# Another order of all steps of the recurrence in a fused RWKV-7 and low-rank mixer kernel

## The chip, the cores and the metric

One Trainium2 chip, of which the kernel uses one core. The metric is the device time of one execution in microseconds (us).

## The reference

Inputs r, k, v, w, a, b have the shape (4, 8, 768, 40): batch, heads, time steps, head size. Per batch and head a 40 x 40 state is carried through the 768 steps, and what comes out is mixed over time by a low-rank pair U, V and over channels by a two-layer network, with a residual sum around each:

```python
for t in range(S):
    y[:, :, t] = einsum('bhd,bhde->bhe', rt, state)
    Sa = einsum('bhde,bhe->bhd', state, at)
    state = state * wt[:, :, None, :] - einsum('bhd,bhe->bhde', Sa, bt)
    state = state + einsum('bhd,bhe->bhde', vt, kt)
x = y.transpose(0, 2, 1, 3).reshape(4, 768, 320)
u = x + ((x.transpose(0, 2, 1) @ U) @ V).transpose(0, 2, 1)      # U 768 x 32, V 32 x 768
out = u + maximum(u @ w_ch1, 0) @ w_ch2                          # 320 -> 1280 -> 320
```

## The kernel before, in words

The recurrence is done in chunks of 64 steps. Two batches share the 128 partitions, so there are 24 chunks ("units"): 0 to 11 for one pair of batches, 12 to 23 for the other. Inside a chunk the steps are turned into matrix products; only one 40 x 40 state per head goes from a chunk to the next. In float32, the work of one chunk n is cut into small steps, each a Python generator that is advanced by one piece at a time:

- W, A, B, V, R, K (load, L370): loads of one input of chunk n, two DMAs of 80 KB. The buffers are few: 3 for V, 2 for each of the others.
- f (prep_f, 7 pieces): clamps w, transposes it on PE (L467), makes running products by two scans on DVE (L530, L538), transposes a, the inverse products and b (L474, L480), and takes scores (L498), of which the two diagonal 32 x 32 blocks go to tiles fl and fh by ACT (L575). L563 is its product on POOL.
- d, g, l, t: the inverse of a unit triangular matrix. d (scatter, L596) stores fl and fh in DRAM with four DMAs, g (gather, L610) reads them back as rows, l (substitute, L626 and L628, 30 pairs of products and sums, some 16 pieces) solves for a whole group of chunks, the last piece of l stores the result (td, L634), and t (fetch, L644 and L647) reads it for one chunk into nT and t2 with four DMAs. The groups are [0], [1, 2, 3], [4 to 7] and so on; group 0 is solved on DVE, the others on POOL.
- s (prep_s): the product of k (POOL, L654), transposes of v, r, k (L474), a DVE transpose of nT (L673), scores (L498) with their masks on DVE (L508), and the two products that complete the triangle (L698, L710).
- c (carry, 7 pieces): the state's chain: L729, L735, eviction, L745, eviction L748, L480, eviction L757, L764, two DVE operations on the state SK (L773, L776), L782, eviction L784.
- o (outputs): L806, L798, L498, L798 and the sum on DVE (L821).
- h: a transpose of running products (L480, L586). q, p (squares, L453): sums of squares of A, B and of V, R, K on ACT, for a check on the size of the inputs.
- w: one piece of the weights' work: a load on SP (L136) into one of two buffers named raw, then integer operations on DVE (L154 to L161, L167) and ACT (L153) and, for most pieces, two products on POOL (L164, L165). m: one piece of the mixer's beginning on chunks 0 to 11 (L181, copies L185 and L186 on DVE and ACT, L191, copies L193).

The string ORDER, 1338 tokens long, says which step is advanced next: "s12" advances s of chunk 12 by one piece. The kernel is recorded in that order, and each engine (PE, DVE, ACT, POOL) and each DMA queue takes its own instructions in it, waiting by semaphores for what it needs. DMAs are issued on SP, or on ACT: a token with an "a" behind it issues all of its DMAs on ACT, with an "x" one half on each; a gather has one queue, which is SP for "x". A DMA that waits for a free buffer or for a landing holds back what stands behind it on its queue, and on ACT that is evictions too. After the list comes part_2 for all chunks (up-projection L268 and L273, down-projection L298), which the change doesn't touch.

Of the kernel before, what the change touches and what calls it, by code (L numbers as in the profile page):

```python
# [37 lines left out]
def kernel(  # L38
# [46 lines left out]
    W2 = []  # L85
# [259 lines left out]
    with ExitStack() as p1:  # L345
# [494 lines left out]

        QUEUES = {"s": (nc.sync, nc.sync), "a": (nc.scalar, nc.scalar), "x": (nc.sync, nc.scalar)}
        ORDER = """
W0x W1x A1 A0x B1 B0a f0 V1a f1 f0 W3x f0 K0x f1 q0 f0 o12 W2 q0 q1 f3 f0 A2 s0 h1 A3 h0 f2 f0 f1 f1 q1 k f2 V2a
f2 f0 W4 V0 f2 f1 B2 f3 d0x K1x W5 R1 q2 q2 s1 f3 f1 g0a f2 f3 f1 f4 B3x q3 f2 f5 d1 l0 l0 f3 l0 f2 A4 B4x h2 f3
f4 q3 d2 f3 g1 f4 l0 d3x s1 f4 h4 l0 f4 p2 p0 R0x g2 p1 q4 q4 p0 f4 A5x l0 p1 l0 l0 s0 h3 l0 A6a q5 f5 g3 s1 f5
B5x l1 l1 l1 l0 s0 l0 f4 W7x p0 f7 l0 l1 q5 W6 d4 R2x f6 s0 o0 l1 h5 p1 l0 f5 l1 B6x l0 A7x W9 s0 K2a q6 q6 f6 l1
l1 f5 p2 l1 p2 l0 W8 s1 l1 B7 f6 w w l0 f5 A8 K3a l0 f5 f7 f6 f6 f7 c0 q7 d5 f6 B8 t0 l1 q8 f7 f7 w l1 f6 d6 h6 l1
A9 g4a f8 s0 f9 s0 g5x l1 f7 c0 l1 f8 l1 s0 f8 f7 d7 s0 h7 c0 o0 l1 A10a g7 f8 o0 c0 g6 c0 V3 s2 f8 l2 W10x t1 l2
t2 c0 s2 o0 s1 c0 s1 w s2 K4 s1 h8 p3 R4 s2 o1 l2 s1 c1 w c1 l2 s1 f8 c1 o1 q10 o1 q9 s2 c1 f10 c1 W12 w o1 q8 c1
W11a R3a s2 q7 l2 B9 s2 f9 l2 s3 f8 s2 d8 c1 s3 l2 c2 f9 s3 f10 l2 l2 s2 c2 f9 l2 s3 h10 f10 t3 s3 g8 c2 w V4 A12x  # L850
f9 s3 s3 c2 h9 s3 w q12 f10 w l2 A11 o2 c2 c2 o2 q9 p3 w p4 B10a o2 l2 c2 f12 f11 l2 l2 l2 c3 c3 V5 W13 q11 s3 l2
B11 f11 p4 o2 f11 w c3 f9 f11 c3 f9 w s4 s4 w o3 d9x o3 s4 p3 o3 l2 c3 f11 K5 A13x t4 o3 w s4 f10 f11 p4 c3 s4 q10
s4 f10 c3 s4 f10 d10x s4 f12 c4 p5 g9 f11 c4 R5 w s5 f12 s4 o4 K6x d11 f12 q11 w h11 c4 B13x o4 g10 o4 w w g11 c4
c4 s5 w t5 s5 R6 s6 o4 s5 s5 V7a c4 s5 s5 V6 l3 f13 s5 W14 l3 l3 c4 w B12 p5 l3 R7 c5 A14 f12 p6 q13 c5 p5 K7 l3
s5 f13 l3 f13 s6 o5 s6 c5 o5 f12 f13 p7 f14 t6 l3 c5 o5 f12 w c5 s6 s6 h12 w d12 p7 o5 c5 s6 t7 W16 p6 q12 W15x s6
s7 f13 l3 f14 p6 l3 w c6 K8a s6 c5 A15 l3 l3 c6 s6 f14 f13 c6 h14 s7 q13 h13 l3 s7 s7 f14 B14x B15 o6 q15 f15 s7
l3 o6 p7 o6 f13 l3 W17 d13x R8 f15 o6 q14 s7 R9 c6 c6 l3 l3 s7 h15 f15 c6 g12a f14 V8 s7 K9 V9 A16a c7 f15 l3 s7
c7 c6 s8 c7 q14 s8 o7 f15 f16 s8 f14 o7 c7 o7 p8 f14 t8 f15 c7 p8 c7 s8 s8 d14 w s9 f15 s8 w c7 g13x d15 g15x o7
g14 p8 s8 f17 c8 s9 s8 f16 p9 t9 l4 c8 s9 s8 V10 f16 s9 c8 o8 l4 K10 l4 s9 R10a A17 f16 p9 s9 c8 l4 R11 o8 c8 s10
q15 V11 s9 B16a q16 c8 p10 t10 o8 f16 s9 q16 l4 s10 o8 c9 w f17 w q17 l4 s10 W18 c9 c8 s9 A18 h16 l4 p11 f17 s10  # L860
p9 W19 A19 f17 c9 B17 o9 o9 f17 s10 w s10 o9 q19 c9 B18x p11 s10 K11 c9 l4 s11 q17 w c9 l4 V12 f16 w l4 s10 c10
t11 c10 f17 f16 s11 l4 f19 o9 s11 l4 s10 s11 R13 p11 h17 c10 f18 c9 s11 s11 d16 l4 s11 c10 B19 K13 q18 g16 f18 f18
A20 l4 s11 c10 o10 o10 W21 W20 q18 c10 o10 p10 l4 p12 w c11 R12 q19 p10 l4 K12x c11 w c10 V14x s12 f18 f17 o10 f19
V13 d17 f18 f19 w p12 l4 p12 s11 s12 o11 f21 o11 A21 w g17x s12 R14 t12 h19 c11 f19 f18 f19 p13 s12 o11 f18 f20
s13 h18 w p13 o11 s12 f19 q20 w s12 d18 s12 f19 K14x f20 d19 B20 s12 s13 s12 s13 f20 c12 c12 f20 g18a f21 g19x c12
f20 s13 c12 c12 f21 q20 l5 t13 f21 o12 w w s14 t14 s13 R15 p13 p14 o12 h20 p14 W23 c12 s14 s13 l5 A22x l5 w s14
o12 w s14 R16 c13 l5 s13 s13 B21 c12 s13 w l5 c13 l5 V15 W22 o13 p14 c13 w l5 w o13 l5 f21 K15 o13 s14 c13 p15 f20
w s14 s14 c13 s15 l5 s15 o13 s15 f22 K16a c13 c14 q21 f22 p15 s14 c13 w s14 t15 c14 p15 B22x w A23 f20 f22 w o14 w
l5 f22 c14 d20 o14 V16 w f21 o14 f22 l5 f21 s15 c14 s15 q21 w d21x f23 c14 f22 s15 w B23x l5 c14 s15 l5 l5 h21 o14
l5 f22 w s15 K17 f23 c14 g20x f23 c15 s16 f23 d22x s15 w R17 l5 w c15 f23 p16 w V17 w c15 o15 s16 w s16 o15 s16 l5  # L870
o15 c15 f23 g22a c15 c15 s17 w t16 p17 g21a s16 f23 w s16 d23x c15 s16 w o15 w V18 p16 s17 s17 s16 c16 c16 s17 w
s16 h23 g23 l6 w w t17 c16 w w p17 p16 w R18 p17 w o16 l6 s17 K18 s17 c16 o16 p18 c16 t18 w l6 s17 l6 p18 s18 c16
s17 l6 o16 q22 w w s18 q23 s18 c17 c17 l6 s17 V19 c16 w s18 s18 w w c17 o16 w s18 w c17 p18 w s18 w o17 l6 c17 c17
K19a l6 w w s18 w o17 c18 w V20 o17 w c18 w s18 c17 R19 c18 o18 p19 s19 p19 o17 w t19x o18 w w p20 l6 o18 s19 l6 w
s19 c18 s19 c18 w K20a w p19 w o18 w s19 w V21 c18 s20 w l6 R20x w p21 w p20 w l6 w l6 s19 s19 l6 K21a R21a w w w
l6 w m l6 s20 s19 w p21 c19 w w c18 s19 l6 c19 w w w o19 w c19 s20 w o19 t20 c19 R22x s20 s20 o19 w w c19 w s20
s20 V22 w w w w q22 w c19 s20 h22 s21 o19 s21 t21 p20 c20 w c11 w w s20 c20 w w w s21 s21 c11 w m c20 w w s21 c19
K22a w w p21 w s21 w o20 s21 o20 c20 o20 w w c20 w w s21 s22 w w c20 V23x s22 t22 o20 s21 s22 w c21 q23 w w w w
c21 w s22 w w m w p22 c21 c20 s22 p23 w s22 R23a t23 w c21 o21 c11 o21 w c21 s22 w w w o21 w w c21 K23 w s23 w c22
w o21 w w s23 s22 c22 s23 s23 s23 w m s22 w w w w c21 w c22 w m s23 o22 w w o22 w w w o22 w c22 w o22 c11 w w c22  # L880
s23 m w w c22 w w w w p23 s23 c23 s23 c23 p22 w m c22 c23 o23 w c23 w w w o23 w w o23 w w c23 o23 w c23 w w w w m
w p22 w w w p23 c23 w
"""
        steps = {"f": F, "s": S, "c": C, "o": O, "h": H, "q": QF, "p": QS, "l": G}
        for x in ORDER.split():
# [39 lines left out]
    p3 = ctx.enter_context(ExitStack())  # L925
# [11 lines left out]
    with tc.If(n_bad > 0) as way:  # L937
        with ExitStack() as p2:
# [3 lines left out]
            g1 = p2.enter_context(tc.tile_pool(name="g1", bufs=1))  # L942
            g2 = p2.enter_context(tc.tile_pool(name="g2", bufs=2))
# [103 lines left out]
```

## Time and profile before

| | |
|---|---|
| median of 6 runs | 764.67 us (757.37 to 776.38) |
| the profiled execution's own time | 765.35 us |
| its span, first to last instruction | 763.5 us |
| mean granted TensorE clock | 0.924 |
| DMAs issued on SP and on ACT in the built program | 627 and 102 |

The page has these parts: busy time of each engine; the span in 40 slices of 19.1 us, with the busy share in tenths and the clock that PE was granted; DMA queues; the chain of work that ended last; groups of instructions by line, with the idle time before them and what ended it; and DMA issues. Other answers of the trace are tables by window, lists of waits, and timelines. [...]

### The profile page before, as it was taken

Reading aid. Unit: us, or ns where it says so; the run is one execution under the profiler, and the core shown is the slowest. Engines: PE = TensorE matmul, PEld = TensorE weight load, DVE = VectorE, ACT = ScalarE, POOL = GpSimd, SP = SyncE. Lnnn points to the kernel's source line nnn. Section 1 sums busy time; section 2 is a strip of 40 time slices with the busy share of each in tenths; the row PEclk is TensorE's granted clock in tenths of the full one; section 3 lists DMA queues with packets and bytes.
Section 4 is the critical chain, followed back from the end, with each engine's and each line's share of the span. In section 5 each row is a group of like instructions: output and inputs, shape, how many; then the busy total and the mean of one; then the engine's idle time right before and its main releaser. Section 6 shows DMA issues by size and latency. Waiting matters only on the chain.

```text
span 763.5 us, 27019 instructions
## 1 busy us (share of the span) xinstructions
PE 696.4 (91%) x11714; PEld 515.7 (68%) x11714; DVE 367.2 (48%) x808; ACT 261.6 (34%) x660; POOL 290.8 (38%) x527
## 2 busy tenths in 40 slices
PE   4755999989998989999977999899999999999997
PEld 3544888878887878888866887456474564746555
DVE  8999558547466467684673775221121212021110
ACT  2562455647555555556433553010100001000000
POOL 6376688168638724973995441000000000000000
PEclk9955699999999797999795999999999999999999
DMA  6764544465556455554433340001010010100101
GB/s 108 127 106 77 113 76 85 98 124 93 111 95 112 78 106 103 93 107 99 92 76 92 90 106 21 7 11 32 0 25 17 17 26 1 33 9 16 26 0 39
DMA packets 216046, 50.53 MB, mean 66 GB/s; under 512 B 207728, under 2 KB 211184, under 8 KB 215920
## 3 DMA queue, kind: packets, MB, share of 16 engines
q1 hardware_dynamic: 170528, 41.04, 27.2%
q10 hardware_dynamic: 45392, 7.69, 5.8%
q8 instruction: 94, 1.54, 0.8%
q14 instruction: 32, 0.26, 0.1%
HBM read 37.68 MB, written 10.22 MB: 63 GB/s over the span
## 4 chain that ended last, share of the span: by engine, by line
PE 78%; DVE 11%; DMA 4%; issue 2%; POOL 2%; ACT 1%; SPq 1%; ACTq 0%; DVEq 0%; POOLq 0%
PE p L298 17%; PE p L268 14%; PE one L798 5%; PE two L498 5%; PE two L764 5%; PE two L474 4%; PE one L480 4%; PE p L273 4%; PE one L729 3%; PE two L782 3%; PE one L735 2%; PE two L745 2%; PE two L710 2%; PE one L806 2%; PE one L467 1%
## 5 line engine op out<-in xcount | busy, mean ns | idle before, releaser
L298 PE MATMUL p<-ip,hid 128*128 128x320 f32 x384 | 107.3, 432 | 0.0
L628 POOL TENSOR_TENSOR ln<-ln,tmp 128x30 f32<-128x30 f32 (+19 forms) x180 | 98.6, 548 | 14.1
L626 POOL TENSOR_TENSOR tmp<-ln 128x30 f32<-128x30 f32 (+19 forms) x180 | 93.7, 521 | 12.6
L298 PEld LDWEIGHTS p<-ip,hid 128*128 128x128 f32 x384 | 73.0, 190 | 30.4
L268 PE MATMUL p<-uf,W 128*128 128x512 f32 x200 | 89.7, 599 | 0.0
L277 ACT ACTIVATE hid<-p 128x512 f32<-128x512 f32 x30 | 17.9, 597 | 206.4 <-PE p L273 170.0
L278 DVE TENSOR_SCALAR hid<-p 128x512 f32<-128x512 f32 x30 | 20.8, 692 | 113.6 <-PE p L273 68.1
L268 PEld LDWEIGHTS p<-uf,W 128*128 128x128 f32 x200 | 36.8, 190 | 50.4 <-issue 50.2
L303 DVE TENSOR_TENSOR o<-p,XTM 128x320 f32<-128x320 f32 x23 | 11.3, 492 | 111.3 <-PE p L298 111.3
L654 POOL TENSOR_TENSOR nKT<-nK,ip 128x320 f32<-128x320 f32 x24 | 22.1, 919 | 41.0 <-PE two L764 23.5
L467 PE MATMUL one<-ID,nWC 128*128 128x128 f32 x96 | 20.1, 346 | 17.4 <-DVE nWC L517 16.1
L508 DVE TENSOR_TENSOR ng<-two,MU 128x512 f32<-128x512 f32 x24 | 16.5, 688 | 38.8 <-PE two L498 38.7
L563 POOL TENSOR_TENSOR nBT<-nB,ip 128x320 f32<-128x320 f32 x24 | 21.5, 895 | 34.5 <-ACT ip L555 32.5
L729 PE MATMUL one<-nV,e 64*64 64x40 f32 x768 | 31.7, 246 | 0.7 <-ACT ip L555 0.5
L729 PEld LDWEIGHTS one<-nV,e 64*64 64x64 f32 x768 | 28.9, 156 | 2.9 <-issue 1.0
L538 DVE TENSOR_TENSOR_SCAN IP<-one,seg 128x511 f32<-128x511 f32 x24 | 30.5, 1272 | 0.0
L530 DVE TENSOR_TENSOR_SCAN PF<-one,seg 128x512 f32<-128x512 f32 x24 | 29.4, 1225 | 2.2
L298 PE MATMUL p<-fa,hid 128*128 128x320 f32 x96 | 29.8, 432 | 0.0
L782 PE MATMUL two<-ID,SK 128*128 128x128 f32 x176 | 27.5, 306 | 2.4 <-DVE SK L776 2.4
L798 PE MATMUL one<-nBT,ng 64*64 64x40 f32 x768 | 28.2, 232 | 1.1 <-DVE ng L508 1.1
L798 PE MATMUL one<-nKT,cm 64*64 64x40 f32 x768 | 28.2, 232 | 0.0
L798 PEld LDWEIGHTS one<-nBT,ng 64*64 64x64 f32 x768 | 25.6, 140 | 3.5 <-DVE ng L508 1.7
(176 smaller groups left out, 1377.6 us busy)
## 6 DMA issues: line engine op xcount, KB each, us to landing
raw<-in_moe_w_ch_dram SPq DMA_DIRECT2D x18, 320.0 KB, 3.6
out_dram<-o SPq DMA_DIRECT2D x46, 80.0 KB, 2.1
nW<-in_w_dram SPq DMA_DIRECT2D x40, 80.0 KB, 3.2
nV<-in_v_dram SPq DMA_DIRECT2D x40, 80.0 KB, 3.2
nA<-in_a_dram SPq DMA_DIRECT2D x36, 80.0 KB, 3.3
nR<-in_r_dram SPq DMA_DIRECT2D x36, 80.0 KB, 3.1
nB<-in_b_dram SPq DMA_DIRECT2D x33, 80.0 KB, 3.1
td<-ln SPq DMA_DIRECT2D x5, 512.0 KB, 3.3
```

The lines of the kernel that those rows point to most:

```text
L268: nc.tensor.matmul(out=ps_[j + x][:], lhsT=W1[i][:, (j + x) * 128:(j + x + 1) * 128], rhs=uf[i], start=start and i == 0, stop=not start an ...
L273: nc.tensor.matmul(out=ps_[j + x][:], lhsT=W1[2][half(x), (j + x) * 128:(j + x + 1) * 128], rhs=uf[2][half(x)], start=start, stop=not start)
L298: nc.tensor.matmul(out=p[:, 0:DM], lhsT=hid[:, f, 2 * j * L:2 * (j + 1) * L], rhs=W2[f], start=(f == 0), stop=(f == NJ - 1))
L474: nc.tensor.transpose(out=p[:, x, off + L * i:off + L * (i + 1)], in_=t[half(x), 2 * i:2 * i + 2, :].rearrange("p h e -> p (h e)"), identi ...
L480: nc.tensor.transpose(out=p[:, 128 * i:128 * (i + 1)], in_=t(i), identity=ID[:])
L498: nc.tensor.matmul(out=p[half(z), s, off + DP * i:off + DP * (i + 1)], lhsT=x(s, i, z), rhs=y(s, i, z), start=True, stop=True)
L626: eng.tensor_tensor(out=x, in0=ln[:, 0:j, j:j + 1].to_broadcast([m, j, n]), in1=ln[:, j:j + 1, j + 1:].to_broadcast([m, j, n]), op=ALU.mult)
L628: eng.tensor_tensor(out=ln[:, 0:j, j + 1:], in0=ln[:, 0:j, j + 1:], in1=x, op=ALU.add)
L729: nc.tensor.matmul(out=p[half(x), D * h:D * (h + 1)], lhsT=u.e[half(x), s, i, :], rhs=vt[half(x), h, 0:D], start=h == 0, stop=first, skip_ ...
L764: nc.tensor.matmul(out=p[:, x, 2 * D * i:2 * D * (i + 1)], lhsT=y[half(x), 2 * i:2 * i + 2, :].rearrange("p s e -> p (s e)"), rhs=z[half(x ...
L782: nc.tensor.transpose(out=p[:, x, 128 * i:128 * (i + 1)], in_=SK[:, x, 2 * i:2 * i + 2, :].rearrange("p s e -> p (s e)"), identity=ID[:])
L798: nc.tensor.matmul(out=py[half(x), D * h:D * (h + 1)], lhsT=m[half(x), s, i, :], rhs=z[half(x), h, 0:D], start=start and h == 0, stop=stop ...
```

## The change: a new ORDER

The list of tokens is replaced by another one with the same steps, the same number of pieces of each (1338 tokens), and other suffixes on some of the DMAs: 117 DMAs are issued on ACT and 612 on SP. No function is changed. Of the 40 lines of each list, those that the prediction speaks of, and the first and last:

```diff
         QUEUES = {"s": (nc.sync, nc.sync), "a": (nc.scalar, nc.scalar), "x": (nc.sync, nc.scalar)}
         ORDER = """
-W0x W1x A1 A0x B1 B0a f0 V1a f1 f0 W3x f0 K0x f1 q0 f0 o12 W2 q0 q1 f3 f0 A2 s0 h1 A3 h0 f2 f0 f1 f1 q1 k f2 V2a
...
-l1 f5 p2 l1 p2 l0 W8 s1 l1 B7 f6 w w l0 f5 A8 K3a l0 f5 f7 f6 f6 f7 c0 q7 d5 f6 B8 t0 l1 q8 f7 f7 w l1 f6 d6 h6 l1
-A9 g4a f8 s0 f9 s0 g5x l1 f7 c0 l1 f8 l1 s0 f8 f7 d7 s0 h7 c0 o0 l1 A10a g7 f8 o0 c0 g6 c0 V3 s2 f8 l2 W10x t1 l2
-t2 c0 s2 o0 s1 c0 s1 w s2 K4 s1 h8 p3 R4 s2 o1 l2 s1 c1 w c1 l2 s1 f8 c1 o1 q10 o1 q9 s2 c1 f10 c1 W12 w o1 q8 c1
...
-c4 s5 w t5 s5 R6 s6 o4 s5 s5 V7a c4 s5 s5 V6 l3 f13 s5 W14 l3 l3 c4 w B12 p5 l3 R7 c5 A14 f12 p6 q13 c5 p5 K7 l3
...
-c7 c6 s8 c7 q14 s8 o7 f15 f16 s8 f14 o7 c7 o7 p8 f14 t8 f15 c7 p8 c7 s8 s8 d14 w s9 f15 s8 w c7 g13x d15 g15x o7
...
-A20 l4 s11 c10 o10 o10 W21 W20 q18 c10 o10 p10 l4 p12 w c11 R12 q19 p10 l4 K12x c11 w c10 V14x s12 f18 f17 o10 f19
-V13 d17 f18 f19 w p12 l4 p12 s11 s12 o11 f21 o11 A21 w g17x s12 R14 t12 h19 c11 f19 f18 f19 p13 s12 o11 f18 f20
...
-s16 h23 g23 l6 w w t17 c16 w w p17 p16 w R18 p17 w o16 l6 s17 K18 s17 c16 o16 p18 c16 t18 w l6 s17 l6 p18 s18 c16
-s17 l6 o16 q22 w w s18 q23 s18 c17 c17 l6 s17 V19 c16 w s18 s18 w w c17 o16 w s18 w c17 p18 w s18 w o17 l6 c17 c17
-K19a l6 w w s18 w o17 c18 w V20 o17 w c18 w s18 c17 R19 c18 o18 p19 s19 p19 o17 w t19x o18 w w p20 l6 o18 s19 l6 w
-s19 c18 s19 c18 w K20a w p19 w o18 w s19 w V21 c18 s20 w l6 R20x w p21 w p20 w l6 w l6 s19 s19 l6 K21a R21a w w w
-l6 w m l6 s20 s19 w p21 c19 w w c18 s19 l6 c19 w w w o19 w c19 s20 w o19 t20 c19 R22x s20 s20 o19 w w c19 w s20
...
-w p22 w w w p23 c23 w
+W0x W1x A0x A1 f0 q0 B1 f1 f0 f0 f0 B0 W2x f2 q1 V0 q1 W3 W4 R0a A2a f1 f0 A3 q0 V2 h0 f1 f2 f0 f1 p0 f1 f0 f3 q2
...
+p2 l0 f6 B7x s1 p1 W9 s1 R3x A7 l0 p1 w l0 o0 l1 f6 f7 f7 l1 c0 B8x q7 s0 l1 d5a c0 t0 f7 f8 g4 s0 g5 f7 h6 f6 q8
+d6 h7 l1 l1 f7 s0 f8 f7 w s0 h8 l1 f8 c0 l1 K3x o0 d7 l1 f8 g7a w c0 W10a o0 c0 s2 f8 g6 l1 l2 q8 w c0 V3a t1 l2
+A9 o0 s2 w c0 s1 t2 s2 s1 s1 o1 s1 B10x c1 R4a p2 f10 l2 c1 w s1 l2 o1 q7 s2 p3 s2 c1 f8 q9 s2 c1 f9 A10 o1 c1 s2
...
+o3 s5 V6x s4 f11 w c3 f10 d10 R6 s4 f12 p5 c4 q12 s4 c4 f12 f11 s4 d11 W15 g9 h11 f12 g11x w p5 t5 o4 c4 w s5 o4
...
+p8 o6 h14 f13 l3 t7x l3 o6 f14 f15 g12 s7 c6 c6 w A16 l3 V9 B15 s7 h13 l3 s7 s7 s7 R9 c6 l3 q16 W17x l3 d13x q14
+f15 c7 s7 p9 c7 f14 c6 f15 w h15 f15 w s8 q15 f14 c7 l3 o7 f15 o7 o7 s8 s8 c7 c7 w f15 s8 d14 c7 t8x s9 g13x V10
...
+s11 c10 h18 l4 l4 p12 l4 w c11 K12 R13x l4 l4 o10 w V13 s11 q19 g16x o10 f18 f20 l4 c11 w f17 w d17x l4 f18 o10
+c10 p11 s12 V14 o10 f19 p12 f19 s11 l4 s12 o11 s12 c11 o11 p13 R14 h19 f18 B20 f19 f21 o11 A20x t12 f19 s12 w f18
...
+o15 f23 g22 c15 f23 o15 w t16 s16 o15 p16 c15 f23 c15 s16 f23 d23x V18 w w w c15 s16 g23 s17 s17 s16 s17 s17 w o15
+w c15 w w c16 l6 s16 s16 c16 w o16 R18 s16 p17 w l6 c16 p18 l6 o16 w t17 s17 c16 R19x w w c16 s17 t18x c16 c17 w
...
+p17 s18 K19a s18 w w o17 h23 c17 c18 o17 s18 c18 c17 s19 s19 w w w w w l6 s19 w w o17 w p19 c18 o18 R20x o18 o18 w
+w c18 t19 c18 w s19 s19 V20 p18 w K20x p19 w w o18 c18 l6 w V21x c11 l6 w w s20 R21 w w s19 w w q23 s19 l6 w l6 w
+w w s19 p20 w m p19 p20 l6 K21x w w w s19 l6 l6 l6 p21 s20 c19 s20 c19 l6 c18 w w w s20 c19 o19 w o19 w w w t20 w
...
+w c23 c23 w p23 o23 o23 w w o23 m w
 """
         steps = {"f": F, "s": S, "c": C, "o": O, "h": H, "q": QF, "p": QS, "l": G}
         for x in ORDER.split():
```

## The prediction

> **What bounds the kernel now.** I read the page first, then a table of 20 us windows, the waits of PE, and the timelines and POOL groups around the two longest stalls.
>
> ```profile
> PE 696.4 (91%) x11714; PEld 515.7 (68%) x11714; DVE 367.2 (48%) x808; ACT 261.6 (34%) x660; POOL 290.8 (38%) x527
> ...
> PE   4755999989998989999977999899999999999997
> ...
> DVE  8999558547466467684673775221121212021110
> ...
> PEclk9955699999999797999795999999999999999999
> ```
>
> There are three stages. Until about 90 us DVE is full and PE is not. From there to 482.4 us, where the chain of waits has the first up-projection group (L268), PE is full with four dents. The 281.1 us after that hold no step of the list and stay. The dents show in narrow windows (columns: window, length, busy PE, PEld, DVE, ACT, POOL, granted clock, DMA share, GB/s):
>
> ```profile
> 282.00:286.00 4.00, 1.36 (x40) 0.99 (x29) 1.09 (x3) 0.04 (x1) 0.00 (x0) 0.94 0.40 62
> 286.00:290.00 4.00, 3.02 (x88) 2.77 (x89) 3.73 (x9) 2.21 (x6) 0.22 (x1) 0.50 0.53 86
> 290.00:296.00 6.00, 6.00 (x87) 4.92 (x86) 4.03 (x12) 2.13 (x6) 0.13 (x1) 0.52 0.73 151
> ...
> 394.00:398.00 4.00, 1.89 (x56) 0.80 (x48) 3.90 (x6) 0.00 (x0) 3.77 (x6) 1.00 0.34 90
> 398.00:402.00 4.00, 0.00 (x0) 0.00 (x0) 2.92 (x5) 1.12 (x4) 3.61 (x7) 0.52 0.37 61
> 402.00:406.00 4.00, 0.48 (x1) 0.48 (x2) 2.82 (x5) 0.81 (x2) 3.53 (x8) 0.50 0.70 149
> ```
>
> A PE wait is followed by half clock for some 10 to 20 us, so a wait costs its length and about as much again. What ended the two longest waits after 100 us, and the first of them in the timeline:
>
> ```profile
> PE one L191 <- DVE fa L185: 9.6, 1, 9.6
> ...
> PE two L698 <- DVE cm L508: 3.9, 2, 3.6
> ```
>
> ```profile
> 280.68 1.10 SPq L644 DMA_DIRECT2D nT<-td  x2
> ...
> 284.91 0.45 DVE L673 STREAM_TRANSPOSE tt<-nT 128x256 f32<-128x256 f32 x1 [3.65 <-DMA nT<-td]
> ...
> 286.98 0.65 PE L698 MATMUL two<-tt,fh 32*32 32x32 f32 x32 [3.62 <-DVE cm L508]
> ```
>
> So the wait at 283 us is the fetch of chunk 12's inverted triangle (t12), issued late on SP: POOL had finished that group at 264.6, and SP stored it at 274.9. The wait at 395 us has two candidates, POOL's work between 387 and 408 us, and ACT held for a load:
>
> ```profile
> L626 POOL TENSOR_TENSOR tmp<-ln 128x234 f32<-128x234 f32 (+12 forms) x13 | 7.7, 593 | 0.9
> L628 POOL TENSOR_TENSOR ln<-ln,tmp 128x238 f32<-128x238 f32 (+13 forms) x14 | 7.4, 528 | 1.1
> L164 POOL TENSOR_TENSOR raw<-raw,unit 128x320 f32<-128x320 f32 x2 | 1.8, 882 | 0.0
> L165 POOL TENSOR_TENSOR raw<-bits,raw 128x320 f32<-128x320 f32 x2 | 1.8, 879 | 0.2
> L654 POOL TENSOR_TENSOR nKT<-nK,ip 128x320 f32<-128x320 f32 x1 | 0.9, 878 | 0.0
> ```
>
> ```profile
> 387.94 8.41 SPq L136 DMA_DIRECT2D raw<-in_moe_w_ch_dram  x3
> 396.45 1.34 SPq L370 DMA_DIRECT2D nV<-in_v_dram  x2
> ```
>
> ```profile
> 400.14 0.47 ACT L453 ACTIVATE sink<-nV 128x320 bf16<-128x320 f32 x1 [7.46 <-DMA nV<-in_v_dram]
> ```
>
> [...] the 7.46 us above held every eviction behind that square. [...] here 32 KB of nT lands in 2.6 us and 512 KB of td in 3.3. [...] here an issue is about 0.65 us on either queue.
>
> **The change.** The same tokens, in another order; the only other difference is which queue issues. From the built programs I add, token by token, each engine's instructions by their durations in this trace (PE groups from start to next start at full clock: L798 1.01, L729 1.06, L764 0.96, a pair of L498 1.09). One chunk is f 2.55, h 0.59, s 3.10, c 5.92, o 3.31 = 15.47 us of PE; 24 chunks, less what first and last ones lack, plus the first m's, 372.9, in both orders. SP issues 15 DMAs fewer, ACT 15 more.
>
> Prologue: DVE work up to a token plus PE work after it, at the worst token: before 76.5 + 343.5 = 420.0 (an f8), after 71.6 + 347.0 = 418.6 (an s0). Change -1.4 us. The traced 482.4 exceeds 420.0 by 62.4: c1's third step comes at 102.1 us with 327.8 us of PE left (429.9), so 9.9 are lost before it and 52.5 after. In the windows after 102 us the clock is low for 58 us, 29 if PE is the bound; 23.5 are left as waits. By place: 395 us, 11 + 10; t12, 3.7 + 5.1; t5 (158 us), 2.7 + 1.7; around 360, 1 + 5; around 240, 3 + 7; the rest small.
>
> First fetch of each group: from POOL's end, td is issued (0.65) and lands (3.3), two nT issues take 1.1, landing 2.6, the transpose 0.45: 8.1 us before L698 needs it. PE work between td's token and that L698, chunks 1, 4, 8, 12, 16, 20: before 9.1, 8.0, 16.2, 11.4, 7.8, 7.6; after 5.4, 10.6, 11.5, 11.2, 13.2, 11.2. Chunk 1 gets 2.7 short: +2.7 us. The others get room.
>
> Other fetches need 4.2 us from t to L698, plus what SP is late. Before, t5 has 3.5 and SP 0.4 late behind it; after, 9.8: its 2.7 + 1.7 go, -4.4. The new thin ones (t17 4.6, t19 4.4, t8 4.7 with half of it on ACT) just fit: +0.5 for one of them late.
>
> t12: before, SP has 22.8 us of issues (35 of 0.65) in a stretch with 15.1 of PE, 7.7 too many, and t12 went out 6.1 us after PE was there. After, the excess around it is 5.3, so some 3.7 late, with 6.7 instead of 8.4 us to L698: 4.2 + 3.7 - 6.7 = 1.2 short, where the same sum gives 1.9 before and the trace 3.6. I keep half: -4.4 of 8.8.
>
> The stall at 395 us: from the weight step ahead of p20 to the first m, 14 pairs of L626/L628, 4 weight products and one L654 are 18.5 us of POOL, against 6.2 of PE: 12.3 too much, and 11 were lost. Behind POOL's products stands DVE's L167, behind it L185, and for that PE's L191. After, from the w ahead of V20 to the first p21, POOL has 18.6 and PE 7.3: 11.3, or 13.7 in the worst part of it. I cost this at 0, bounds -1 and +2. What would take the cover away is K20, now right behind a weight load on SP; POOL waits for it with l6 behind.
>
> ACT's 15 issues (9.8 us) lie in its idle time (34% busy); uncovered they cost 9.8. The gather g7 now stands on ACT with no PE work between it and d7 (2.8 before, on SP): at most four issues and a landing, 2.6 + 2.5 = 5.1 us, in which ACT evicts nothing; I take 0 here, since DVE is the later engine there.
>
> Sum: -1.4 + 2.7 - 4.4 + 0.5 - 4.4 + 0 = -7.0 us on a span of 763.5, so 756.5. That execution took 765.35 (1.85 around the span) against a median of 764.67, so 756.5 + 1.85 - 0.7 = 757.7.
>
> **The rivals.** (1) Not POOL but the load was the cause at 395 us: V21 stood behind a weight fetch that waited 7 us, and p21 1.0 us of PE after it. After, 4.9 us and 35 tokens lie between. Then the 21 us go too: 757.7 - 21 = 737. For it: ACT's 7.46 us. Against: POOL busy 88 to 94% through the whole stall.
> (2) Slower: ACT waits in front of evictions. Each DMA that ACT must hold back stops the PSUM evictions behind it; priced like t12, 3.7 + 5.1 = 8.8 us. The place is g7 behind d7, at 85 to 95 us, in chunk 0's state chain (L748, L757, L784), then t8's and K20's halves. It decides from two such events: 757.7 + 17.6 = 775; three give 784. Against it: ACT is 34% busy.
> (3) Nothing: the gains are given back by other thin places (SP's worst excess is now 8.9 us around d14, t8, d15, against 7.7), since the lost 52.5 us come from an order that already fits closely: 764 to 768. Also that the change doesn't do what it is for: the prologue's sum moves by 1.4 us alone.
>
> **How the numbers follow.** Forecast 0.50, itself 748 to 765; (1) 0.17; (2) 0.25; (3) 0.08. Faster by over 1% means below 757.0 (about what a measurement of this kernel can tell from no change, with runs from 757 to 776): half of the forecast's 0.50 and all of (1), 0.42. Within 1%: the other half and (3), 0.33. Slower: 0.25. The range leaves out the lower half of (1), 0.08, and the upper part of (2), 0.12: 738 to 780.
>
> **What would show it.** Right: no L673 wait on nT over 2 us between 100 and 380 us; mean clock above 0.93; a PE wait of some 11 us remains between the last l6 steps and the first m, with POOL over 85% busy. Rival (1): that wait is under 4 us. Rival (2): ACT idle over 3 us on ln<-fd or a load, and PE short in the same window. Wrong altogether: the first c1 after 108 us, or dents where no fetch is late.

## The result and the profile after

| | before | after |
|---|---|---|
| median of all runs (lowest to highest) | 763.76 us (754.26 to 776.38, 71 runs) | 756.95 us (748.79 to 767.61, 34 runs) |
| ratio to before, 95% interval | | 0.9927 [0.9905, 0.9948] |
| profiled execution, its span | 765.35 us, 763.5 | 764.69 us, 763.0 |
| its granted clock | 0.924 | 0.926 |

The change makes the kernel 0.7% faster, within the 1% that the text on record named as the limit. The profiled execution of the changed kernel was one of its longer ones (the median of its runs has a clock of 0.938), so the two profiles have the same span: I compare them stage by stage, and kernels of the experiments that share a part of an order serve as repeats. A slip in the text ahead of the prediction: both lists have 1336 tokens, not 1338.

The page of the kernel after, the same lines as of before:

```profile
PE 688.7 (90%) x11714; PEld 510.7 (67%) x11714; DVE 373.0 (49%) x808; ACT 259.6 (34%) x660; POOL 290.8 (38%) x527
...
PE   4654799989999989999967989899999999999997
...
PEclk9855599998999998799995999999999999999999
```

PE is full from the sixth digit on, one later than before, and the 21st digit (the stall near 395 us) is as low as it was, 6 against 7. To see where the time went I cut both traces at the L745 of certain chunks, and split each stage into PE's work, its idle time, and half of what it was busy at half clock (in us; "lost" is the sum of the last two):

| stage | length before | after | lost before | after | lost, 3 kernels with the old order from chunk 1 on (t5 or t12 moved, or p21) | lost, kernels with the new one there |
|---|---|---|---|---|---|---|
| start to chunk 1 | 102.1 | 109.3 | - | - | | |
| chunk 1 to 4 | 49.7 | 46.7 | 1.9 | 0.6 | 3.4 to 4.7 | 0.2 to 2.9 |
| 4 to 8 | 67.2 | 70.3 | 5.4 | 8.2 | 7.3 to 8.8 | 2.2 to 8.2 |
| 8 to 12 | 74.2 | 62.3 | 16.8 | 4.7 | 13.5 to 18.4 | 1.8 to 5.6 |
| 12 to 16 | 62.5 | 67.3 | 3.2 | 9.2 | 4.2 to 8.7 | 3.2 to 5.8 |
| 16 to 20 | 74.6 | 73.9 | 23.2 | 20.9 | 23.0 to 24.0 | 18.7 to 23.0 |
| 20 to first L268 | 52.2 | 53.8 | 3.7 | 7.5 | 3.7 to 3.8 | 8.0 to 10.5 |

(The last column leaves out the kernels that edit the stall at 395 us, in the row 16 to 20, and in the row 4 to 8 e9, whose seam lies there.) Three differences hold in all repeats, but for one kernel in the second (e2, below). The first stage is longer: 108.5 to 109.3 us in the three kernels that leave the new start as it is, against 101.1 to 105.7 with the old one. The stage from chunk 8 to 12 loses 8 to 17 us less. The end loses 4 to 7 us more. The profile of after has 10.2 us of half clock from 311.5 us on, behind a PE wait of 1.05 us, which together cost 6 us between 12 and 16; a stretch of that size is in none of the others with this order.

The stage from chunk 8 to 12 as one window, of before and then of after (window, length, busy PE, PEld, DVE, ACT, POOL, granted clock, DMA share, GB/s):

```profile
219.00:293.10 74.10, 67.18 (x1738) 58.98 (x1736) 43.42 (x100) 39.05 (x105) 41.02 (x75) 0.86 0.57 104
```

```profile
226.20:288.60 62.40, 59.90 (x1724) 52.53 (x1720) 42.91 (x96) 36.76 (x100) 41.34 (x74) 0.97 0.57 105
```

Nearly the same number of matmuls takes 67.2 us of PE at a clock of 0.86, and 59.9 at 0.97 (times the clock, 57.8 and 58.1, which is why half of the busy time at half clock counts as lost). Cut once more, at single chunks, the stage has two dents (a PE wait and the half clock behind it). The one at 240 us, which the prediction only listed ("around 240, 3 + 7"), is gone: from chunk 9 to 11 before loses 9.0 us and after nothing. The one at t12, which it priced, shrank: from chunk 11 to 12 the loss is 6.9 us before and 4.7 after. Timeline of before at 240 us, ACT and then PE:

```profile
241.94 0.47 ACT L453 ACTIVATE sink<-nA 128x320 bf16<-128x320 f32 x1 [3.69 <-DMA nA<-in_a_dram]
```

```profile
242.88 1.12 PE L764 MATMUL two<-nx,nBT 64*128 64x80 f32 x16 [1.95 <-ACT nx L757]
```

A square of a (a q token) stood on ACT ahead of the eviction L757 and waited 3.69 us for its load; PE waited 1.95 us for nx, and the clock was at half from 244.6 to 258.2 us. After, no clock below full is granted between 178.4 and 284.2 us. At t12 the wait for the fetched triangle is gone, but a second wait stood right behind it in before, hidden by it. ACT waited 4.45 us to write fl again, until an earlier scatter of it had landed:

```profile
285.96 0.38 ACT L575 ACTIVATE fl<-two 128x256 f32<-128x256 f32 x1 [4.45 <-DMA fd<-fl]
```

After, the same ACT instruction waited 4.57 us, to 282.78, and PE waited 1.9 us for its fh, at the same L698 as before. What ended PE's longest waits from 100 us on, after:

```profile
PE one L191 <- DVE fa L185: 11.8, 1, 11.8
PE two L474 <- POOL nKT L654: 2.7, 2, 2.2
PE two L698 <- ACT fh L575: 1.9, 1, 1.9
PE two L498 <- issue: 1.7, 2, 1.1
PE two L698 <- DVE tt L673: 1.6, 1, 1.6
```

The wait at the first m is still there, and longer than the 9.6 us of before. The windows over it:

```profile
394.00:398.00 4.00, 0.00 (x0) 0.00 (x0) 1.73 (x3) 2.40 (x8) 3.84 (x6) 0.86 0.35 59
398.00:402.00 4.00, 0.00 (x0) 0.00 (x0) 2.43 (x5) 1.79 (x6) 3.61 (x6) 0.50 0.40 102
402.00:406.00 4.00, 0.27 (x1) 0.28 (x2) 1.15 (x2) 0.00 (x0) 3.69 (x7) 0.50 0.00 0
```

POOL is busy 90 to 96%, and no other engine over 61%.

The first stage starts later. The trace of after, in order of time on POOL, SP, POOL and DVE (in the trace of before the last of these starts at 30.43 us with no wait):

```profile
27.36 0.86 POOL L563 TENSOR_TENSOR nBT<-nB,ip 128x320 f32<-128x320 f32 x1 [6.53 <-DMA nB<-in_b_dram]
```

```profile
32.45 0.32 SPq L610 DMA_DIRECT2D ln<-fd  x1
```

```profile
34.81 1.26 POOL L617 TENSOR_SCALAR_AFFINE_SELECT ln<-ln 32x1024 f32<-32x1024 f32 x1 [2.45 <-DMA ln<-fd]
```

```profile
36.10 0.19 DVE L626 TENSOR_TENSOR nRH<-ln 32x30 f32<-32x30 f32 x1 [2.58 <-POOL ln L617]
```

b of chunk 2 came late, and behind POOL's product of it stood the constants and the mask (L617) of group 0, which DVE needed to begin its substitution. But the mask then waited another 2.45 us for its own rows: the gather g0 went out on SP at 32.45 us, behind the loads of V, K and U, where before it went out on ACT at 24.95. No run changes that gather alone.

The substitution of group 0 is also longer: 30.4 to 70.4 us before, 36.1 to 80.7 after, so 5.7 us of later start and 4.7 us of longer duration. The same 60 instructions (L626, L628) take 26.1 us of DVE before and 30.2 after, while POOL is busy beside them for 24.3 and 32.0 us. In the trace of before, a 32x168 product took 0.67 us at 61.85 us beside POOL's work, and the sum of the same size behind it 0.32 us, when POOL had all but stopped.

### The profile page after: what moved, and what is told of

Its sections match the earlier page's. It is cut to its first block, busy times and chain, and to the rows that moved or that the text cites. A ratio compares the mean times of both kernels' runs of the same rounds, so it can differ in the third digit from the quotient of the medians.

```text
span 763.0 us, 27028 instructions
## 1 busy us (share of the span) xinstructions
PE 688.7 (90%) x11714; PEld 510.7 (67%) x11714; DVE 373.0 (49%) x808; ACT 259.6 (34%) x660; POOL 290.8 (38%) x527
## 4 chain that ended last, share of the span: by engine, by line
PE 77%; DVE 9%; POOL 4%; DMA 4%; issue 3%; ACT 1%; SPq 1%; ACTq 0%; POOLq 0%; DVEq 0%
PE p L298 17%; PE p L268 14%; PE one L798 5%; PE two L498 5%; PE two L764 5%; PE one L480 4%; PE two L474 4%; PE p L273 4%; PE one L729 3%; PE two L782 3%; PE two L745 2%; DVE nRH L626 2%; PE one L735 2%; DVE ln L628 2%; PE two L710 2%
## 5 line engine op out<-in xcount | busy, mean ns | idle before, releaser
L628 POOL TENSOR_TENSOR ln<-ln,tmp 128x30 f32<-128x30 f32 (+19 forms) x180 | 100.2, 557 | 14.1
L626 POOL TENSOR_TENSOR tmp<-ln 128x30 f32<-128x30 f32 (+19 forms) x180 | 93.1, 517 | 12.4
L298 PEld LDWEIGHTS p<-ip,hid 128*128 128x128 f32 x384 | 73.0, 190 | 30.4
L268 PE MATMUL p<-uf,W 128*128 128x512 f32 x200 | 89.7, 599 | 0.0
L268 PEld LDWEIGHTS p<-uf,W 128*128 128x128 f32 x200 | 36.8, 190 | 50.4 <-issue 50.2
L508 DVE TENSOR_TENSOR ng<-two,MU 128x512 f32<-128x512 f32 x24 | 16.5, 687 | 34.2 <-PE two L498 33.5
L729 PE MATMUL one<-nV,e 64*64 64x40 f32 x768 | 30.1, 240 | 1.6 <-DVE e L508 1.2
L702 ACT ACTIVATE GX<-two 32x256 f32<-32x256 f32 x48 | 18.1, 376 | 31.2 <-PE two L698 30.5
```

Of the source, the lines that this page charges most:

```text
L268: nc.tensor.matmul(out=ps_[j + x][:], lhsT=W1[i][:, (j + x) * 128:(j + x + 1) * 128], rhs=uf[i], start=start and i == 0, stop=not start an ...
L298: nc.tensor.matmul(out=p[:, 0:DM], lhsT=hid[:, f, 2 * j * L:2 * (j + 1) * L], rhs=W2[f], start=(f == 0), stop=(f == NJ - 1))
L626: eng.tensor_tensor(out=x, in0=ln[:, 0:j, j:j + 1].to_broadcast([m, j, n]), in1=ln[:, j:j + 1, j + 1:].to_broadcast([m, j, n]), op=ALU.mult)
L628: eng.tensor_tensor(out=ln[:, 0:j, j + 1:], in0=ln[:, 0:j, j + 1:], in1=x, op=ALU.add)
L729: nc.tensor.matmul(out=p[half(x), D * h:D * (h + 1)], lhsT=u.e[half(x), s, i, :], rhs=vt[half(x), h, 0:D], start=h == 0, stop=first, skip_ ...
```

## The experiments

My theories at the start: the new order loses in its first stage and gains later; the stall at the first m is POOL's, and its products (L164, L165) are a part of it. The rivals: the stall is ACT's, held by a load (rival 1 on record), or DVE's own queue. All kernels compute the whole reference. Each line's ratio is to the kernel before in the same job; the last two columns are explained with the last experiment.

| kernel | median (runs) | ratio [95%] | c1's L745 | lost 8 to 12 | last step of group 6 | from it to the end |
|---|---|---|---|---|---|---|
| before | - | 1 | 102.1 | 16.8 | 408.2 | 355.3 |
| after | 756.95 (34) | 0.9927 [0.9905, 0.9948] | 109.3 | 4.7 | 410.1 | 352.9 |
| e1 old start, new rest | 755.27 (6) | 0.9900 [0.9841, 0.9959] | 103.4 | 1.8 | 399.6 | 356.7 |
| e2 new start, old rest | 771.77 (22) | 1.0107 [1.0075, 1.0140] | 108.5 | 6.3 | 412.6 | 355.4 |
| e3 products on DVE | 757.07 (22) | 0.9903 [0.9874, 0.9932] | 114.5 | 4.8 | 402.0 | 356.2 |
| e4 p21 later, in before | 765.44 (22) | 0.9969 [0.9932, 1.0006] | 101.1 | 13.5 | 413.8 | 355.2 |
| e5 B2 earlier, in after | 760.34 (22) | 0.9959 [0.9926, 0.9993] | 106.9 | 4.2 | 403.2 | 356.4 |
| e6 weights behind m, in after | 761.31 (22) | 0.9982 [0.9957, 1.0008] | 109.0 | 5.5 | 408.3 | 354.2 |
| e7 t5 earlier, in before | 769.83 (22) | 1.0074 [1.0042, 1.0105] | 103.2 | 18.4 | 415.9 | 355.0 |
| e8 t12 earlier, in before | 770.22 (22) | 1.0054 [1.0017, 1.0090] | 103.2 | 15.5 | 413.8 | 355.2 |
| e9 old to token 500 | 766.84 (22) | 1.0018 [0.9985, 1.0051] | 102.2 | 5.6 | 416.1 | 355.9 |
| e10 old to token 800 | 768.79 (22) | 0.9994 [0.9957, 1.0031] | 105.7 | 15.0 | 412.0 | 356.3 |
| e11 old start, all mended | 758.61 (12) | 0.9905 [0.9868, 0.9942] | 104.6 | 2.5 | 399.3 | 361.8 |
| e12 the same, substitution undisturbed | 747.29 (6) | 0.9797 [0.9747, 0.9847] | 101.3 | 3.1 | 389.9 | 355.2 |

**The start and the rest apart (e1, e2).** The first 250 tokens of one order, then the other order's tokens without what has been done. e1 against before, then e2 against after, at the seam:

```diff
 c1 o1 q10 o1 q9 s2 c1 f10
-c1 W12 w o1 q8 c1 W11a R3a s2 q7
+R3x q8 w B10x w q7 s2 c1 s2 l2
...
```

```diff
 o1 q7 s2 p3 s2 c1 f8 q9
-s2 c1 f9 A10 o1 c1 s2 l2 l2 s3
+f9 A10a K4 q10 o1 c1 c1 W12 o1 c1
...
```

> The first 250 tokens of the list before (up to chunk 1's third state piece), then the remaining tokens in the new list's order. Theory A (the new order loses in the prologue, wins after it): c1's third piece returns from 109 to about 102 us, the rest keeps the new order's fewer waits: about 750 us, 6 below the new kernel. Theory B (my sum: the prologues differ by +1.3 us only): about 756. [...]

> The mirror image: the new list's first 250 tokens, then the rest in the order of before. Theory A: the later prologue with the old waits: about 770 us, and c1's third piece at about 109 us. Theory B: 764 to 765. [...]

Measured: e1 0.9900, e2 1.0107. With the old rest the new start costs 8 us; the new rest gains 8 us behind the old start, and 14 behind the new one. The first stage ends at 108.5 us in e2 and at 103.4 in e1. Whether the changed kernel would keep its gain or better it with the old start isn't settled by e1: its interval holds the 0.9927 of after.

**The products of the weight pieces on DVE (e3).**

```diff
-            todo = dst, raw, nc.vector if n < 8 else nc.gpsimd
+            todo = dst, raw, nc.vector
```

> The new kernel with the two products of every weight piece (L164, L165) on DVE instead of POOL; nothing else moves. Theory A (the wait of PE for L185 is POOL's backlog in group 6, with L167 behind POOL's products): the wait at the first m falls from 11.8 us to under 3, and with it the low clock behind it; 735 to 747 us. Rival (a late load holds ACT there): the wait stays at 10 us or more, 756 to 760 us.

The wait at L191 fell from 11.8 to 7.5 us, not under 3. POOL was relieved, but stood still in the middle of the substitution, behind the product of k of chunk 20, for a load:

```profile
389.34 0.86 POOL L654 TENSOR_TENSOR nKT<-nK,ip 128x320 f32<-128x320 f32 x1 [5.12 <-DMA nK<-in_k_dram]
```

DVE meanwhile stood idle for 0.29 us at most at a time, from 376 us to L185 at 394.86 us: weight pieces of 4 to 6 us each stood ahead of it. So DVE's queue was the last link, for this kernel at least.

**The squares of chunk 21 one place later, in before (e4).**

```diff
-w l6 R20x w p21 w p20 w l6
+w l6 R20x w w p20 w l6
...
-c19 K22a w w p21 w s21 w o20
+c19 K22a w w p21 p21 w s21 w o20
```

> The kernel before, with chunk 21's squares one place later each: the square of V21 stands where that of R21 stood, so that ACT no longer stands behind V21's load ahead of the first m. Theory A (POOL's backlog): PE's wait for L185 stays at 9 to 12 us, 762 to 765 us. Rival (ACT held by V21's load was the cause): the wait falls under 4 us, about 743 us.

ACT no longer stands behind V21 there, and the wait at L191 is 9.0 us. That doesn't test rival 1, for ACT met the same kind of wait again, at the next square:

```profile
405.88 0.47 ACT L453 ACTIVATE sink<-nR 128x320 bf16<-128x320 f32 x1 [6.92 <-DMA nR<-in_r_dram]
```

The trace of after settles it for that kernel. There ACT had copied its part of what L191 needs (L186) by 398.3 us, and the wait went on for over 7 us until DVE's part came at 405.19, right behind this DVE instruction, which waited for POOL's product:

```profile
404.52 0.75 DVE L167 SCALAR_TENSOR_TENSOR W<-raw 128x320 f32<-128x320 int32 x1 [4.02 <-POOL raw L165]
```

So with ACT free the stall stays, and rival 1 falls.

**One load of the start (e5).**

```diff
-q0 V2 h0 f1
+q0 B2 V2 h0 f1
...
-K1a B2 f3
+K1a f3
```

> The changed order, with one token moved: the load of b of chunk 2 (B2) goes out ahead of the second load of v and of the scatter of chunk 0, instead of behind them. Theory: the late B2 is what costs the changed order its first stage (POOL waited 6.5 us for it at 27.4 us, and group 0's rows and the constants stood behind that); then that wait falls under 3 us, group 0's substitution on DVE begins 3 to 4 us before 36.1 us, the first L745 of chunk 1 comes at 104 to 106 us instead of 109.3, and the time is 3 to 5 us under the changed kernel: 752 to 754. Rival: the first stage is set by DVE's amount of work ahead of chunk 1, whatever one load does; then L745 of chunk 1 stays at 108 to 110 us and the time at 756 to 758.

Half of it came: the substitution of group 0 began at 34.3 us instead of 36.1, c1's L745 at 106.9 instead of 109.3. The time isn't better than that of after. B2 is one cause of the late start. For the rest the traces point to the gather g0, which went out at 30.7 us here, and to the longer substitution (45.2 us here, 44.6 in after, 39.9 in before); no run tests these.

**The weight pieces behind the first m (e6).**

```diff
-V21x c11 l6 w w s20 R21 w w s19 w w q23 s19 l6 w l6 w w w s19 p20 w m
+V21x c11 l6 s20 R21 s19 q23 s19 l6 l6 s19 p20 m
...
```

(The 12 w are spread over the 50 tokens behind the first p21.)

> The changed order, with the 12 weight pieces between the load of v of chunk 21 and the first m moved behind that m and spread over the 50 tokens from the first squares of chunk 21 on. Theory: the stall ahead of L191 is a matter of DVE's queue: weight pieces that wait for POOL's products, or fill DVE by themselves, stand ahead of L185; then the wait of L191 falls from 11.8 to under 4 us, no wait over 3 us takes its place, and the time is 10 to 20 us under the changed kernel: 737 to 747. Rival: POOL's sum (its substitution steps and products) is the bound, whatever DVE's queue holds; then a wait of 6 us or more comes back within 20 us of it, at an instruction that needs POOL's nKT or the fetched triangle of chunk 20 or 21, and the time stays at 754 to 758.

The wait at L191 fell to 1.3 us, as the theory had it, but the rival had the rest: a wait of 8.6 us came 10 us later, and the time is 4 us worse than that of after. Its chain in four lines of the trace, POOL, SP, ACT, PE:

```profile
408.12 0.15 POOL L631 MEMSET ln<- 128x32 f32 x1
```

```profile
408.30 0.34 SPq L634 DMA_DIRECT2D td<-ln  x1
```

```profile
412.39 0.50 ACT L153 ACTIVATE raw<-raw 128x320 f32<-128x320 uint32 x1 [10.40 <-DMA raw<-in_moe_w_ch_dram]
```

```profile
413.44 1.12 PE L480 MATMUL one<-ID,xf 128*128 128x128 f32 x4 [8.62 <-ACT XTM L586]
```

POOL finishes group 6 at 408.3 us. SP had its store in hand since 394.8 us, with the weight loads behind it; ACT waited for one of these ahead of an eviction, and PE for that. Take the wait out of DVE's queue, and it comes back through SP's and ACT's: this points to POOL's sum as the cause, and to chance for the queue that passes it on; e12 tests it. (The wait didn't come at nKT or nT, where I had expected it; by the prediction's sum for a first fetch, nT of chunk 20 would have been next, some 8 us behind POOL's end.)

**The two fetches of the prediction, moved in before (e7, e8).**

```diff
-w t5 s5
+w s5
...
-K6x d11
+K6x t5 d11
```

```diff
-R12 q19
+R12a q19
...
-V14x s12
+V14a s12
...
-V13 d17
+V13a d17
...
-o11 A21 w g17x s12 R14 t12 h19
+t12 o11 A21 w g17x s12 R14 h19
```

> The order before, with one token moved: the fetch of chunk 5's triangle (t5) 17 tokens earlier, ahead of the scatter of chunk 11. Theory of the prediction: its wait and the low clock behind it were worth 4.4 us; no wait over 1 us is left between 150 and 170 us, and the time is 759 to 761 where the kernel before has 764. Rival: what is gained there is lost in the next thin place, since the later dents are set by other fetches and by the weight pieces: 763 to 765.

> The order before, with the fetch of chunk 12's triangle (t12) 6 tokens earlier, ahead of a load of a, a gather and a load of r, and three loads ahead of it (r of 12, v of 13 and 14) issued on ACT instead of SP: nT is then issued about 5 us earlier than at 280.7 us. Theory of the prediction: the wait of 3.6 us and the low clock behind it were worth 8.8 us, of which the change was to give half; with all of it gone the time is 755 to 757. Rival: the time is lost again behind it, or ACT's loads hold evictions: 762 to 768, with a low-clock stretch at 280 to 300 us all the same.

Both were slower, by 5.7 and 4.1 us. In both the wait that I had aimed at went (e8's L698 waited 0.29 us), and another came in its place: in e7 3.0 us of PE for POOL's nBT, 13 us further on; in e8 one transfer further down SP's queue, on ACT and then PE:

```profile
290.91 0.38 ACT L575 ACTIVATE fl<-two 128x256 f32<-128x256 f32 x1 [6.24 <-DMA fd<-fl]
```

```profile
291.62 0.69 PE L474 MATMUL two<-ID,nV 64*128 64x64 f32 x8 [4.75 <-ACT fh L575]
```

In e7 t5 now stood ahead of a gather, which went out at 160.0 us instead of 155.3; POOL's substitution of that group began at 167.1 instead of 160.6, and the product nBT stood in it. In e8 SP waited 2.7 us with t12 for the landing of td, time that the loads of before had filled; so the scatter behind went late, ACT waited to write fl again (6.2 us, where before had 4.45), and PE for ACT. These are the waits that the two profiles show. Where the 4 to 6 us of the medians go, they don't: in the profiles the stages 4 to 8 and 8 to 12 last 69.3 and 75.2 us in e7, 70.0 and 73.5 in e8, and 69.5 and 71.1 in e4, which has the list of before up to there.

**Where in the list the gain lies (e9, e10).**

Both against before, at their seams:

```diff
 l3 s7 s7 f14 B14x B15 o6 q15
-f15 s7 l3 o6 p7 o6 f13 l3 W17 d13x
+R8 q14 V8 p8 p7 f16 K9 o6 w W18
...
```

```diff
 t13 f21 o12 w w s14 t14 s13
-R15 p13 p14 o12 h20 p14 W23 c12 s14 s13
+c11 p14 h20 c11 p13 l5 W22x o12 B21 l5
...
```

> The order before for its first 500 tokens (through the fetch of chunk 5's triangle, to about 190 us), the changed order for the rest. From the runs so far the changed order loses some 6 us up to chunk 1 and gains some 13 between there and the first L268. If the gain lies in the first third of that (the fetch t5 and the stretch around it, 250 to 500), this kernel keeps none of it: 764 to 766. If it lies later (the stages from chunk 8 to 12 differ by 10 us between the two orders), this kernel has all of it and none of the loss: 752 to 756.

> The order before for its first 800 tokens (past the fetch of chunk 12's triangle, to about 290 us), the changed order for the rest. If the gain lies between tokens 500 and 800 (the stage from chunk 8 to 12, with t12), this kernel has none of it: 763 to 766. If it lies behind them (the thin fetches, the weight pieces and the first m), it has it: 753 to 758. The prediction's own terms give 764.7 here, since it put both of its gains, t5 and t12, ahead of token 800.

e10 keeps none of the gain: it lies ahead of token 800, where the prediction had put it. e9 is spoilt as a whole: its seam made a stall of its own, with 19.4 us lost between chunk 4 and 8 where before loses 5.4. But its stage from chunk 8 to 12 loses 5.6 us, like the changed order's, and e10's 15.0, like the old one's. So tokens 500 to 800 save that stage. (e2 doesn't fit: with the old tokens it loses 6.3 there, after 9.8 between 4 and 8.)

**What sets the end (e11, e12).** In every kernel so far the span ended 353 to 357 us after the last step of group 6's substitution, and that took 49 to 53 us from its first step, with POOL busy for 46.9 of 51.7 us in after. Alone this proves little, since what delays POOL may delay all the rest. The two kernels shorten that stretch. e11 is e1 with e3's and e6's edits; e12 is e11 with

```diff
-            todo = dst, raw, nc.vector
+            todo = dst, raw, nc.vector if n < 15 else nc.gpsimd
...
-V21x c11 l6 s20 R21 s19 q23 s19 l6 l6 s19 p20 m
+V21x c11 l6 l6 l6 s20 R21 s19 q23 s19 s19 p20 m
```

> The order before for its first 250 tokens, the changed order for the rest, with the products of all weight pieces on DVE instead of POOL, and the 12 weight pieces ahead of the first m moved behind it and spread. Theory: the stall at 395 to 410 us is POOL's sum (group 6's substitution with the products between its steps), passed on to PE by whatever stands in DVE's, SP's or ACT's queue behind it; with the products off POOL the last substitution step ends 8 us earlier, and with the weight pieces behind m DVE doesn't hold L185. Then no wait over 4 us is left between 340 and 420 us and the time is 740 to 748. Rival: DVE, which now has the products, becomes the bound of that stretch and of the weight pieces behind it: 752 to 758, with a wait of 6 us or more at an instruction that needs a DVE result.

> As the kernel with the old start and all mended, with two further edits: only the first 15 weight pieces have their products on DVE (those behind group 6's substitution are on POOL again), and two tokens of that substitution stand ahead of the product of k of chunk 20, for which POOL had waited 5.5 us in the middle of it. In all kernels so far, apart from that one, the end of the span came 353 to 357 us after the last step of group 6's substitution on POOL, and that substitution took 49 to 53 us from its first step. Theory: this stretch of POOL is the path that sets the end. It now takes 43 to 44 us instead of 48.5 (or 52.4 in the kernel with the old start alone), so its last step comes some 8 us earlier, at 391 to 394 us, the span ends 354 to 357 us later, and the time is 747 to 751, some 1.7% under the kernel before. Rival: the substitution only runs along with something else that sets the end; then its last step comes earlier, the distance from it to the end grows to 361 us or more, and the time stays at 755 to 760.

e11 missed: its last step came at 399.3 us, no earlier than e1's 399.6, for POOL had again waited in the middle, and behind the store on SP the chain of e6 came back:

```profile
386.98 0.86 POOL L654 TENSOR_TENSOR nKT<-nK,ip 128x320 f32<-128x320 f32 x1 [5.53 <-DMA nK<-in_k_dram]
```

```profile
404.45 1.11 PE L480 MATMUL one<-ID,xf 128*128 128x128 f32 x4 [7.50 <-ACT XTM L586]
```

It was also 4 us longer from the first L268 on (285.1 us instead of 281.1), for a reason that the profile leaves open: 1.4 us are half clock, and 2.4 lie between the last matmul and the landing of the last store. In e12 the substitution runs from 347.4 to 389.9 us, 42.5 instead of e1's 52.4; first and last step of the two kernels start together (347.35 and 347.24 us) and end apart:

```profile
389.74 0.16 POOL L631 MEMSET ln<- 128x32 f32 x1
```

```profile
399.46 0.16 POOL L631 MEMSET ln<- 128x32 f32 x1
```

The first is e12's, the second e1's. e12's span ends 355.2 us later, as the theory had it, at 745.1; its longest PE wait from 100 us on is 2.9 us. Its time of 747.29 us is 2.0% under before and about 1.3% under after: the fastest kernel of this study. So in e1's order POOL's stretch for group 6 sets the end; a part of e12's gain on e1 is not this stretch, as its c1 came 2.1 us earlier. For before and after the same is inferred from the equal distance to the end; no run shortens the stretch in their own lists.

## Why the prediction was right or wrong

The total was right, -7.0 forecast and -6.8 us measured, and a part of its mechanism; but its terms were off in both directions and made up for each other.

- **Prologue, -1.4, with the first fetch, +2.7: wrong.** Together +1.3 were forecast, and c1's L745 came 7.2 us later (108 us was named as the sign that the whole is wrong; it was 109.3). The failed step is the prologue's sum: it counted what DVE has to do up to a token, not what DVE has to wait for. From 33.5 to 36.1 us DVE stood still behind POOL, which had waited first for b of chunk 2, with 22 issues ahead of it on SP, and last for the rows of g0. The sum also took each instruction at its duration in the trace of before, and group 0's substitution came out 4.7 us longer beside a busier POOL. The first fetch itself cost nothing: PE waited 0.4 us at most for anything between 85 and 126 us.
- **t5, -4.4: wrong.** The stage from chunk 4 to 8 lost 5.4 us before and 8.2 after, with 2.2 to 9.8 in all kernels of either order but e9. I had taken the room between t5 and L698 in PE work (9.8 us) and no lateness of SP. SP was late: a gather ahead of it held the queue 2.2 us.

```profile
160.70 2.22 SPq L610 DMA_DIRECT2D ln<-fd  x2
162.97 0.92 SPq L644 DMA_DIRECT2D nT<-td  x2
```

```profile
165.84 0.45 DVE L673 STREAM_TRANSPOSE tt<-nT 128x256 f32<-128x256 f32 x1 [6.25 <-DMA nT<-td]
```

DVE waited 6.25 us for nT, PE 1.6. That also breaks the sign "no L673 wait on nT over 2 us".
- **t12, -4.4 of 8.8: right in place, too large.** The wait for t12 went, but its place (chunk 11 to 12) lost only 2.2 us less, for ACT's wait behind the scatter, 4.45 us before and 4.57 after, stood behind it and had no term. The stage around it lost 12.1 us less, and 9.0 of these are the dent at 240 us, for which the list of losses had 10 us and the sum nothing. That dent is rival 1's mechanism (ACT held by a square), only not at 395 us where I looked for it. So the agreement of the total is in part luck: the largest gain is one that the sum doesn't have, and it paid for the late start and for t5.
- **Thin fetches, +0.5: right**; no PE wait of over 2 us is at one.
- **The stall at the first m, 0 with bounds of -1 and +2: right.** The wait went from 9.6 to 11.8 us with POOL at 90 to 96%, its stage from 74.6 to 73.9. The reading of POOL's sum was right too: e6 and e11 agree with it, and e12 shows it. What I didn't see is what it means: I priced this stall as one dent of 21 us among others, while in e1's order it sits on the path that sets the end, and by the equal distances in before and after too. The risk named there (k of chunk 20) was real: 5.1 and 5.5 us of POOL in e3 and e11.
- **ACT's 15 issues and g7, 0:** no PE wait longer than 2 us names either.
- **Not forecast:** some 4 to 7 us more lost behind chunk 20, in all kernels with the new ending (7.5 to 10.5, against 3.7), with one PE wait of 2.2 us for POOL's nKT at 443.9 us and 3.4 us of half clock after it in the profile of after.
- **Rival 1** (737 us) fell with the trace of after: ACT was free and the stall stayed. **Rival 2** (ACT waits ahead of evictions) came in a small way after the change, not where it was looked for: ACT's 4.57 us for the scatter and PE's 1.9 us behind it. It is also what e8 ran into. **Rival 3**, that gains are given back at other places, is what happened in e7 and e8, and in part here.

## What to carry to other kernels

In this kernel a wait that ended at a queue was seldom that queue's: of five edits that took away a named wait of PE (e6, e7, e8, e11, e12), four got another wait in its place, and the one that paid shortened the busy engine behind it. So look for the stretch in which one engine is about 90% busy while all others wait, and for what interrupts it; check that an edit hasn't swapped a wait for the same one a step later (e4); and count, for a moved transfer, what stands ahead of it on its queue and what it will stand in front of. A sum that agrees with the measurement says little about its terms: cut both traces into stages with the same work and compare these, with other kernels as repeats.

## What the runs showed of the hardware

- One execution of a kernel differs from the next by up to 2.5% (748.8 to 767.6 us for the same program), and the time goes with the mean clock: of the changed kernel's runs, those with a clock 0.01 higher are about 4 us shorter (a straight line through 36 runs). With this spread one profile can't show a gain of 1%. The change as a whole shows in the clock: the medians are 0.929 and 0.938.
- Instructions of DVE took longer beside POOL's work: in e11 L164 on DVE took 0.90 and 0.81 us while POOL substituted (to 399.3 us), and 0.48 when it had ended, so up to 0.4 us more; L154, which has one input, took 0.65 and 0.33. Group 0's 60 small instructions on DVE agree: 26.1 us in all before and 30.2 after, with POOL busy beside them for 24.3 and 32.0 us. So moving POOL's products to DVE gave DVE more than 0.5 us for some of them. No run shows the cause.
- What a wait of PE cost in half clock varied from case to case. The text on record speaks of some 10 to 20 us behind a wait; from 100 us on, the two traces have these stretches at a clock of 0.50:

| trace | half clock from | its length | PE waits just ahead of it, or under way |
|---|---|---|---|
| before | 162.7 us | 3.4 us | 1.29 and 1.25 us |
| before | 244.6 | 13.6 | 1.95 |
| before | 285.6 | 10.2 | 3.62 |
| before | 364.1 | 10.2 | 0.92 and 0.72 |
| before | 398.2 | 20.5 | 9.63 |
| before | 483.5 | 3.4 | 2.08 |
| after | 168.2 | 10.2 | 1.59 and 1.02 |
| after | 284.2 | 6.8 | 1.86 |
| after | 311.5 | 10.2 | 1.05 |
| after | 396.9 | 20.5 | 11.8 |
| after | 444.7 | 3.4 | 2.16 |

- Loads on ACT's queue held an eviction in e8: the issue of two DMAs of v took 2.44 us of its queue from 271.54 us on, and the eviction L575 behind them started at 274.10 us, after 1.86 us of idle time.
